# Two heads' row maxima side by side on TensorE, and one softmax shift for a pair of heads

## The chip, the cores and the metric

The kernel runs on one core of a Trainium2 chip. Its engines are TensorE (PE in the profile; PEld is its loading of weights), VectorE (DVE), ScalarE (ACT), GpSimd (POOL) and SyncE (SP, which here only issues DMAs). The metric is the time of one execution on the device, in microseconds, as the median of several runs.

## The reference

Attention with pooled queries is followed by a gated unit with a spatial product. B = 8, H = 8, 1152 keys, head size 64; two neighbouring queries are averaged, so there are 576 query rows.

```python
def _attn_ref(q, k, v):
    q_pool = q.reshape(B, H, S // 2, 2, D).mean(axis=3)
    scores = (1.0 / np.sqrt(D)) * np.matmul(q_pool, k.transpose(0, 1, 3, 2))
    scores = scores - np.max(scores, axis=-1, keepdims=True)
    attn = np.exp(scores)
    attn = attn / (np.sum(attn, axis=-1, keepdims=True) + 1e-09)
    return np.matmul(attn, v)

def _moe_ref(x, w_in, w_spatial, b_spatial, w_out):      # x: (8, 576, 512), heads joined
    h = np.maximum(x @ w_in, 0.0)
    u, v = h[..., :512], h[..., 512:]
    v_n = (v - mean(v)) / np.sqrt(var(v) + 1e-06)        # over the last axis
    v_s = np.einsum('ts,bsd->btd', w_spatial, v_n) + b_spatial[None, :, None]
    return (u * v_s) @ w_out
```

## The kernel before

**Pairs.** Two heads of a batch are worked on together as a pair; there are 32 pairs. A head's 576 query rows are cut into a main part of 512 and a tail of 64. Keys stand in 9 chunks of 128. Float32 precision is kept with float16 operands split into a high and a low part (`xq` or X, `khi`, `qhi`, `klo` or KL, `kn`; three sets of each, `kn` in one buffer).

**`prep(i)`** scales and splits queries and keys of pair i. X holds the high part of the queries, lower 64 partitions for head 0 and upper 64 for head 1; `kn` the high part of the keys in the same way. DMAs then copy them into `qhi` and `khi`, where a head's high and low parts lie over all 128 partitions; two small ones fill `qd`, a block-diagonal tile with the tails of both heads. `lnp` is the offset that the shift gets.

**`maxima(i)`** finds the largest score of each query row ahead of the exponentials. There are 9 row tiles (`t` 0 to 3 are head 0's main part, 4 both tails, 5 to 8 head 1's main part), each in three products of 128 query rows with 384 keys (L617; L608 for the tails). Each product goes to a PSUM bank, `pm` (two buffers) or `pw` (two buffers), of which `pw` is used only while no gated unit is running. VectorE reduces each (L623).

**`shift`** turns 4 or 5 columns of maxima into rows: a reduction (L635), the subtraction of `lnp` (L636), a transpose on TensorE (L640), the split in two float16 rows (L642, L643) and two DMAs into partitions 64 and 65 of X (L648). It is called twice for a pair, after tile 4 and after tile 8. Those two rows take part in the second score product: `products` multiplies the high parts (L793, 128 rows) and then KL with X (L794, 66 rows), which adds the low part of the keys and subtracts the shift.

**`attention(i)`** runs over 18 steps (2 heads, 9 chunks). In each, a score tile `pss` (L793, L794) goes through the exponential on ScalarE (L799) into one of 8 `pt` buffers, GpSimd splits it (L811), and two steps later `values` multiplies it with the values (L713, L717, L722; 12 small products a step). Tails are 64 columns wide and go through `tail_tile` and `tail_values`. While attention(i) runs, `maxima(i + 1)`, the values of the next pair, `prep(i + 2)` and the weights are advanced by generators.

**`gated_unit`** is the second half of the reference, for two batches at a time (L868 to L1058). A unit runs beside the next eight pairs; the last one runs alone at the end.

**Order.** Class `Order` records every instruction and its accesses, and `pin` then fixes each engine's order by list scheduling with a table of costs: the instruction that can start first, and among those the first in the program. The engines work through that order in sequence.

Of the kernel before, what the change touches and what calls it, by code (L numbers as in the profile page):

```python
# [10 lines left out]
F16 = mybir.dt.float16  # L11
# [20 lines left out]
class Order:  # L32
# [144 lines left out]

    def two_from_sbuf(self, ins):
        if ins.opcode not in ("TensorTensor", "TensorScalarPtr", "TensorCopy"):
            return False  # L180
        return not any(self.slot.get(x.bass_ap.tensor.name, (0, 0))[1] for x in ins.ins if hasattr(x, "bass_ap"))

    def pin(self, tc):
# [22 lines left out]
        cost = [self.cost(e, i) for e, i in zip(lane, prog)]  # L206
        shared = [e in ("DVE", "Pool") and self.two_from_sbuf(i) for e, i in zip(lane, prog)]
# [4 lines left out]
        wire = 0.0  # L212
# [3 lines left out]
        for _ in prog:  # L216
            best = None
            for e, ns in ready.items():
                if ns:
# [42 lines left out]
def attn_sgu_kernel(ctx: ExitStack, tc: tile.TileContext, qT, kT, v, w_in, w_spT, b_sp, w_out, out):  # L262
# [27 lines left out]
    pp = order.pool(ctx.enter_context(tc.tile_pool(name="pp", bufs=8)), 8)  # L290
# [35 lines left out]

    qd = [const.tile([P, 2, TAIL], F16, name=f"qd{i}") for i in range(2)]
    for t in qd:
        nc.gpsimd.memset(t, 0.0)

# [204 lines left out]
    def prep(i):  # L535
# [19 lines left out]
        nc.vector.scalar_tensor_tensor(  # L555
            out=lnp, in0=s[:, 0:1], scalar=math.log(PEXP) / ESC, in1=s[:, 1:2], op0=ALU.mult, op1=ALU.mult
        )
        nc.vector.tensor_scalar_min(lnp, lnp, 2.0 ** 29)
# [35 lines left out]
    def maxima(i):  # L594
        st = state[i]
        qhl, khh, X = st["qhl"], st["khh"], st["X"]
        W = KEYS // 3
        NB = W // P
        mt = sm.tile([P, NT, 3], F32, name="mt", bufs=2)
        for t in range(NT):  # L600
            for n in range(3):

                if units or (t + n) % 2:
                    pm = ps_m.tile([P, 512], F32, name="pm")
                else:
                    pm = ps_w.tile([P, 512], F32, name="pw")
                if t == 4:
                    nc.tensor.matmul(  # L608
                        pm[:, :W],
                        lhsT=qd[i % 2].rearrange("p h s -> p (h s)"),  # L610
                        rhs=st["kn"][:, n * NB : (n + 1) * NB, :],
                        start=True, stop=True,
                    )
                else:
                    h = 0 if t < 4 else 1
                    c0 = t * P if t < 4 else TAIL + (t - 5) * P
                    nc.tensor.matmul(  # L617
                        pm[:, :W],
                        lhsT=qhl[:, h, c0 : c0 + P],
                        rhs=khh[:, h, n * NB : (n + 1) * NB, :],  # L620
                        start=True, stop=True,
                    )
                nc.vector.reduce_max(out=mt[:, t, n : n + 1], in_=pm[:, :W], axis=AX.X)  # L623
                yield

            if t == 4:
                yield from shift(st, mt, 0, 5)
        yield
        yield from shift(st, mt, 5, NT)

    def shift(st, mt, a, z):
# [4 lines left out]
        nc.vector.tensor_scalar_sub(mx[:, :n], mx[:, :n], st["lnp"])  # L636
# [5 lines left out]
        nc.vector.tensor_scalar_mul(mr[:n, 0], pt[:n, :P], 1.0 / MROW)  # L642
        nc.vector.scalar_tensor_tensor(  # L643
# [532 lines left out]
```

## Time and profile before

| | |
|---|---|
| median of 3 runs | 1245.7 us (1244.05 to 1246.76) |
| the profiled execution | 1241.88 us, of which its span is 1240.1 us |
| mean granted TensorE clock | 0.979 |
| PE, DVE, ACT, POOL busy | 94%, 76%, 71%, 70% |
| chain that ended last | PE 70%, DVE 13%, ACT 3% |

"Busy" is a mean over stretches that differ. The prediction uses three of them: from 30 to 285 us pairs are worked on without a gated unit, from 285 to 1137 us with one, and from 1137 us the last unit runs alone. Matmuls are pipelined: a matmul's duration in the profile is longer than the distance to the next one's start, so distances between starts are read from the timeline.

### The profile page before, as it was taken

To read this page: it belongs to the slowest core of one execution; us is meant where nothing else is said; L and a number is where in the kernel's file an instruction comes from. 1 tells how busy PE (TensorE), PEld (TensorE's weight loads), DVE (VectorE), ACT (ScalarE), POOL (GpSimd) and SP (SyncE) were. 2 spreads that over 40 slices of the span, in tenths; PEclk is the share of its full clock that TensorE was granted. 3 is DMA by queue.
4 is the path that set the end of the run, shared out by engine and by line. 5 is a ranking of instruction groups with operands and counts; after the bars stand their busy time and mean duration, and the time that the engine had idled before them with its cause. 6 is when DMAs were issued, how large, how long until landed. Compare 5 with 4: busy or idle time off the path is not lost.

```text
span 1240.1 us, 34103 instructions
## 1 busy us (share of the span) xinstructions
PE 1165.3 (94%) x13632; PEld 732.9 (59%) x13632; DVE 941.6 (76%) x2219; ACT 885.1 (71%) x1627; POOL 872.4 (70%) x750
## 2 busy tenths in 40 slices
PE   3878879789999999999999999999999999999998
PEld 1555556556666666566666666666665666665454
DVE  5689999998878777876679777876669867841644
ACT  4677669778977787868677887768777786754333
POOL 2768969799878777778787777778877776774000
PEclk9879899899999999999999999999999999999999
DMA  5454364336333533155323432246332321110002
GB/s 186 161 167 137 90 199 120 110 90 198 92 109 78 147 112 104 53 137 165 106 74 93 131 95 68 74 128 186 109 91 74 90 70 50 33 44 36 1 1 77
DMA packets 62335, 126.70 MB, mean 102 GB/s; under 512 B 13728, under 2 KB 21920, under 8 KB 61664
## 3 DMA queue, kind: packets, MB, share of 16 engines
q1 hardware_dynamic: 62176, 124.52, 34.1%
q8 instruction: 107, 1.75, 0.6%
q14 instruction: 52, 0.43, 0.1%
HBM read 81.20 MB, written 9.44 MB: 73 GB/s over the span
## 4 chain that ended last, share of the span: by engine, by line
PE 70%; DVE 13%; ACT 3%; issue 2%; POOL 2%; DMA 1%; ACTq 0%; DVEq 0%; SPq 0%; POOLq 0%
PE pss L793 8%; PE pss L794 8%; PE pm L617 7%; PE pw L868 6%; PE pw L973 6%; PE pw L1016 6%; DVE mt L623 5%; PE pw L932 5%; PE o L713 4%; PE o L722 4%; PE o L717 4%; ACT pt L799 1%; PE pss L868 1%; PE pss L973 1%; DVE vv L372 1%
## 5 line engine op out<-in xcount | busy, mean ns | idle before, releaser
L811 POOL TENSOR_TENSOR pt<-pt 128x512 f16<-128x512 f32 x576 | 637.1, 1123 | 206.4 <-ACT pt L799 204.7
L799 ACT ACTIVATE pt<-pss,esc 128x512 f32<-128x512 f32 x576 | 387.1, 686 | 164.3 <-PE pss L794 122.4
L623 DVE TENSOR_REDUCE mt<-pm 128x1 f32<-128x384 f32 x733 | 385.7, 547 | 60.6 <-PE pm L617 52.4
L793 PE MATMUL pss<-qhi,khi 128*128 128x64 f16 (+1 forms) x1152 | 270.7, 289 | 13.5 <-ACT pt L799 11.2
L794 PE MATMUL pss<-xq,klo 66*128 66x64 f16 (+1 forms) x1152 | 275.8, 290 | 1.5 <-DMA xq<-mr 1.5
L713 PE MATMUL o<-vp,pt 128*128 128x65 f16 x2304 | 229.6, 196 | 0.0
L717 PE MATMUL o<-vp,pt 128*128 128x64 f16 x2304 | 227.6, 194 | 0.0
L617 PE MATMUL pm<-khi,qhi 128*128 128x384 f16 x655 | 206.0, 331 | 14.5 <-DVE mt L623 8.1
L713 PEld LDWEIGHTS <-pt 128*128 128x128 bf16 x2304 | 179.9, 99 | 46.6 <-issue 6.3
L717 PEld LDWEIGHTS <-pt 128*128 128x128 bf16 x2304 | 169.4, 99 | 31.7 <-issue 2.4
L722 PE MATMUL o<-vp,pt 128*128 128x65 f16 x2304 | 172.2, 195 | 0.9 <-POOL pt L811 0.7
L722 PEld LDWEIGHTS <-pt 128*128 128x128 f16 x2304 | 121.6, 99 | 26.2 <-POOL pt L811 4.0
L794 PEld LDWEIGHTS <-klo 66*128 66x128 f16 x1152 | 98.3, 99 | 51.5 <-issue 22.4
L617 PEld LDWEIGHTS <-qhi 128*128 128x128 f16 x768 | 74.7, 99 | 83.3 <-issue 36.2
L793 PEld LDWEIGHTS <-khi 128*128 128x128 f16 x1152 | 99.8, 99 | 30.7 <-issue 7.3
L868 PE MATMUL pw<-wi_h,xg 128*128 128x512 f16 x240 | 89.0, 378 | 0.0
L811 POOL TENSOR_TENSOR ptl<-ptl 128x1152 f16<-128x1152 f32 x32 | 71.3, 2230 | 19.6 <-ACT ptl L807 19.5
L807 ACT ACTIVATE ptl<-pss,esc 128x256 f32<-128x256 f32 (+1 forms) x128 | 63.7, 498 | 29.8 <-PE pss L794 29.4
L932 PE MATMUL pw<-xg,wi_h 128*128 128x512 f16 (+1 forms) x336 | 82.8, 325 | 0.0
L973 PE MATMUL pw<-ws_h,vv 128*128 128x512 f16 x216 | 80.5, 379 | 0.3 <-DVE u L983 0.3
L1016 PE MATMUL pw<-wo_h,vv 128*128 128x512 f16 x216 | 79.7, 379 | 0.8 <-DVE vv L372 0.8
L623 DVE TENSOR_REDUCE mt<-pw 128x1 f32<-128x384 f32 x131 | 70.1, 543 | 11.0 <-PE pw L617 10.5
(190 smaller groups left out, 2335.4 us busy)
## 6 DMA issues: line engine op xcount, KB each, us to landing
vt<-in_v_dram SPq DMA_DIRECT2D x56, 576.0 KB
qt<-in_qT_dram SPq DMA_DIRECT2D x32, 576.0 KB
kt<-in_kT_dram SPq DMA_DIRECT2D x32, 576.0 KB
khi<-kn SPq DMA_DIRECT2D x128, 144.0 KB
out_dram<-row SPq DMA_DIRECT2D x24, 256.0 KB
qhi<-xq SPq DMA_DIRECT2D x64, 72.0 KB
klo<-klo SPq DMA_DIRECT2D x32, 144.0 KB
vv<-in_w_in_dram SPq DMA_DIRECT2D x4, 1024.0 KB
```

Of the source, the lines that this page charges most:

```text
L617: nc.tensor.matmul(pm[:, :W], lhsT=qhl[:, h, c0 : c0 + P], rhs=khh[:, h, n * NB : (n + 1) * NB, :], start=True, stop=True,)
L623: nc.vector.reduce_max(out=mt[:, t, n : n + 1], in_=pm[:, :W], axis=AX.X)
L713: nc.tensor.matmul(o[:, t], lhsT=top[:, cols], rhs=vp[:, D : D + D1], start=c == 0 and t == 0, stop=False, skip_group_check=True,)
L717: nc.tensor.matmul(o[:, t, 0:D], lhsT=top[:, cols], rhs=vp[:, 0:D], start=False, stop=False, skip_group_check=True)
L722: nc.tensor.matmul(o[:, t], lhsT=rst[:, cols], rhs=vp[:, D : D + D1], start=False, stop=c == NC - 1, skip_group_check=True,)
L793: nc.tensor.matmul(o, lhsT=khh[:, h, c, :], rhs=qhl[:, h, q], start=True, stop=False)
L794: nc.tensor.matmul(o, lhsT=KL[0:KR, h, c, :], rhs=X[0:KR, h, q], start=False, stop=True)
L799: nc.scalar.activation(pt, ps, AF.Exp, bias=0.0, scale=esc)
L811: nc.gpsimd.tensor_sub(t.bitcast(F16)[..., 0::2], t, t.bitcast(BF16)[..., 1::2])
L868: nc.tensor.matmul(ph, lhsT=xa[:, cc, c0 : c0 + P], rhs=wa[:, cc, DH:DF], start=n == 0, stop=n == 3 * NCC - 1,)
L973: nc.tensor.matmul(pv, lhsT=l, rhs=r[:, 0:MAIN], **fl)
L1016: nc.tensor.matmul(py, lhsT=ga[:, fc, c0 : c0 + P], rhs=wa[:, fc, :], start=m == 0, stop=m == end - 1)
```

## The change

Six edits that go together:

1. Ahead of the maxima, the products read X and `kn` directly: 64 rows (the high part of the queries) where they had 128 (high and low part). For pairs 1 to 31, a product of head 0 (rows 0 to 63 of the array) and one of head 1 (rows 64 to 127) are issued one behind the other into two banks. For the tails both write one bank, 64 partitions each. Pair 0 keeps its products one at a time, and its two shifts. `qd` and its DMAs are gone; `kn` has two buffers, `pt` seven in place of eight.
2. The tails come first, then tiles 0 and 5 together, 1 and 6, and so on; `shift` is called once for all nine columns, at the end.
3. In `shift`, `lnp` is subtracted behind the transpose, on the row in PSUM; the split takes a copy and a subtraction.
4. `lnp` is made by an activation and one VectorE instruction in place of two on VectorE.
5. In `values` and `tail_tile`, the products into the same columns stand four or five apart and no longer next to each other.
6. `Order` learns that such products belong together: the first waits in the plan for what the second needs, the second follows at once, and the first is planned with 60 ns.

```diff
+        side = {
+            n - 1: n for n in range(1, len(prog))
+            if self.rows(prog[n - 1]) == (0, 64) and self.rows(prog[n]) == (64, 128)
+        }
+        for a, b in side.items():
+            before[a] |= before[b]
+            begun[a] |= begun[b] - {a}
+            begun[b].add(a)
...
+        for a in side:
+            cost[a] = (60, cost[a][1] + 60)
...
+            if beside is not None:
+                best = (free["PE"], "PE", beside)
             t, e, n = best
+            beside = side.get(n)
...
-    pp = order.pool(ctx.enter_context(tc.tile_pool(name="pp", bufs=8)), 8)
+    pp = order.pool(ctx.enter_context(tc.tile_pool(name="pp", bufs=7)), 7)
...
-        nc.vector.scalar_tensor_tensor(
-            out=lnp, in0=s[:, 0:1], scalar=math.log(PEXP) / ESC, in1=s[:, 1:2], op0=ALU.mult, op1=ALU.mult
+        nc.scalar.activation(lnp, s[:, 0:1], AF.Copy, bias=0.0, scale=s[:, 1:2])
+        nc.vector.tensor_scalar(
+            out=lnp, in0=lnp, scalar1=math.log(PEXP) / ESC, scalar2=2.0 ** 29, op0=ALU.mult, op1=ALU.min
         )
-        nc.vector.tensor_scalar_min(lnp, lnp, 2.0 ** 29)
...
-        for h, (a, rows) in enumerate(((MAIN, lower), (0, upper))):
-            nc.sync.dma_start(out=qd[i % 2][rows, h], in_=X[rows, 0, a : a + TAIL])
-        kn = st["kn"] = ld.tile([P, NC, P], F16, name="kn")
+        kn = st["kn"] = ld.tile([P, NC, P], F16, name="kn", bufs=2)
...
+        def product(o, h, c0, m, n):
+            nc.tensor.matmul(
+                o[:, :W],
+                lhsT=X[halves[h], 0, c0 : c0 + m],
+                rhs=kn[halves[h], n * NB : (n + 1) * NB, :],
+                start=True, stop=True,
+            )
+        def tails(n):
+            o = bank(n % 2)
+            for h in range(2):
+                product(o[halves[h]], h, MAIN * (1 - h), TAIL, n)
+            largest(4, n, o)
...
+        for n in range(3):
+            tails(n)
+            yield
+        for t in range(4):
+            for n in range(3):
+                os = [bank(h) for h in range(2)]
+                for h, o in enumerate(os):
+                    product(o, h, first(t + 5 * h), P, n)
+                for h, o in enumerate(os):
+                    largest(t + 5 * h, n, o)
+                    yield
+        yield
+        yield from shift(st, mt, 0, NT)
...
         nc.vector.reduce_max(out=mx[:, :n], in_=mt[:, a:z], axis=AX.X)
-        nc.vector.tensor_scalar_sub(mx[:, :n], mx[:, :n], st["lnp"])
...
-        nc.vector.tensor_scalar_mul(mr[:n, 0], pt[:n, :P], 1.0 / MROW)
-        nc.vector.scalar_tensor_tensor(
-            out=mr[:n, 1], in0=pt[:n, :P], scalar=1.0 / MROW, in1=mr[:n, 0], op0=ALU.mult, op1=ALU.subtract
+        m = pt[:n, :P]
+        nc.vector.tensor_scalar(
+            out=m, in0=m, scalar1=st["lnp"][:n], scalar2=1.0 / MROW, op0=ALU.subtract, op1=ALU.mult
         )
+        nc.vector.tensor_copy(out=mr[:n, 0], in_=m)
+        nc.vector.tensor_sub(mr[:n, 1], m, mr[:n, 0])
...
                 o[:, t], lhsT=top[:, cols], rhs=vp[:, D : D + D1], start=c == 0 and t == 0, stop=False,
                 skip_group_check=True,
             )
+        for t in range(4):
+            cols = slice(t * P, (t + 1) * P)
             nc.tensor.matmul(
                 o[:, t, 0:D], lhsT=top[:, cols], rhs=vp[:, 0:D], start=False, stop=False, skip_group_check=True
             )
```

What this makes of the order is shown at two places. The first is TensorE's order in the second stretch, inside a step of `values`, as it was. `pt` is the stationary operand of the value products, `qhi` that of a product for the maxima.

```order
L713 LDWEIGHTS pt
L713 MATMUL o<-vp_99,pt 128x65
L717 LDWEIGHTS pt
L717 MATMUL o<-vp_99,pt 128x64
L617 LDWEIGHTS qhi_117
L617 MATMUL pm<-khi_114,qhi_117 128x384
L713 LDWEIGHTS pt
L713 MATMUL o<-vp_99,pt 128x65
L717 LDWEIGHTS pt
L717 MATMUL o<-vp_99,pt 128x64
```

The same kind of place in the new order (L757 and L763 are what L713 and L717 were, L625 a product for the maxima; each product still has its own load of weights ahead of it):

```order
L757 LDWEIGHTS pt
L757 MATMUL o<-vp_100,pt 128x65
L625 LDWEIGHTS xq_112
L625 MATMUL pm<-kn,xq_112 128x384
L625 LDWEIGHTS xq_112
L625 MATMUL pm<-kn,xq_112 128x384
L757 LDWEIGHTS pt
L757 MATMUL o<-vp_100,pt 128x65
L757 LDWEIGHTS pt
L757 MATMUL o<-vp_100,pt 128x65
```

Two products for the maxima, both into `pm`, now stand one behind the other among value products, and L757 follows L757 where L717 stood between. Such products stand in exactly twos at 392 places of the new order, between instructions of full height, and in fours at 30.

The second place is VectorE's order in the first stretch, around a shift. Before (`mx` are the maxima, `mr` the rows made of them; L387, L372 and L555 belong to the weights, to `prep` and to `lnp`):

```order
L635 TENSOR_REDUCE mx<-mt 128x5
L555 SCALAR_TENSOR_TENSOR lnp<-qks 128x1
L636 TENSOR_SCALAR mx<-mx,lnp 128x5
L558 TENSOR_SCALAR lnp<-lnp 128x1
L642 TENSOR_SCALAR mr<-pm 5x128
L372 SCALAR_TENSOR_TENSOR qhi_118<-qt,qks,xq_112 128x576
L643 SCALAR_TENSOR_TENSOR mr<-pm,mr 5x128
```

And now (L678 is what L635 was; L685, L688 and L689 follow the transpose; L388, L412 are other work of `prep` and of the weights):

```order
L678 TENSOR_REDUCE mx<-mt 128x9
L388 SCALAR_TENSOR_TENSOR klo_106<-kt,qks,kn 128x512
L685 TENSOR_SCALAR pm<-pm,lnp 9x128
L412 TENSOR_TENSOR u<-u,vv 128x1024
L688 CAST mr<-pm 9x128
L633 TENSOR_REDUCE mt<-pm 128x1
L689 TENSOR_TENSOR mr<-pm,mr 9x128
```

The instruction with `lnp` stands behind the transpose and works on PSUM, all nine columns pass in one go, and other work stands between the three instructions of the row.

More of the change, by code (lines that the diff above doesn't have):

```diff
@@ L595, in maxima @@
         st = state[i]
-        qhl, khh, X = st["qhl"], st["khh"], st["X"]
+        X, kn = st["X"], st["kn"]
         W = KEYS // 3
         NB = W // P
+        halves = (slice(0, D), slice(D, P))
         mt = sm.tile([P, NT, 3], F32, name="mt", bufs=2)
-        for t in range(NT):
-            for n in range(3):
[L603 to L627, printed above, removed]
@@ new lines, in tails, with first @@
+        def tails(n):
[3 more added lines that the diff above has]
+            largest(4, n, o)
+        def first(t):
+            return t * P if t < 4 else TAIL + (t - 5) * P
+        if i == 0:
+            for t in range(NT):
+                for n in range(3):
+                    if t == 4:
+                        tails(n)
+                    else:
+                        o = bank((t + n) % 2)
+                        product(o, t // 5, first(t), P, n)
+                        largest(t, n, o)
+                    yield
+                if t == 4:
+                    yield from shift(st, mt, 0, 5)
+            yield
+            yield from shift(st, mt, 5, NT)
+            return
```

31 lines of the change are left out of this document (24 added, 7 removed).

## The prediction, made before the changed kernel was run

> **What bounds the kernel now.** I read the windows first, because the mean hides three stretches.
>
> ```profile
> 0.00:30.00 30.00, 10.01 (x32) 3.84 (x32) 17.22 (x43) 12.91 (x27) 7.57 (x16) 0.93 0.58 192
> 30.00:285.00 255.00, 214.39 (x2747) 141.98 (x2747) 230.13 (x500) 191.50 (x346) 206.75 (x162) 0.91 0.45 136
> 285.00:1137.00 852.00, 841.63 (x10262) 538.20 (x10259) 642.75 (x1558) 643.47 (x1184) 658.10 (x573) 1.00 0.34 98
> 1137.00:1241.00 104.00, 99.24 (x603) 48.85 (x598) 51.46 (x121) 37.25 (x72) 0.00 (x0) 1.00 0.08 26
> ```
>
> The columns are PE, PEld, DVE, ACT, POOL, clock, DMA. From 30 to 285 us VectorE is the busiest (230 of 255); from 285 to 1137 TensorE is busy 842 of 852 and the others 643 to 658; the last 104 us are the unit alone, which the change doesn't touch. A busy PE could still hide waits, so the waits of TensorE in the second stretch come next, then the timeline, which shows whether products follow each other as fast as they stream.
>
> ```profile
> PE pm L617 <- DVE mt L623: 4.2, 9, 1.1
> PE pm L617 <- DVE xt L771: 2.5, 3, 0.8
> PE pm L617 <- DVE rs L900: 1.0, 3, 0.4
> ```
>
> Its largest waits are 7.7 us together. So there each nanosecond of stream that goes is time, and in the first stretch a nanosecond of VectorE.
>
> ```profile
> 399.96 0.27 PE L640 MATMUL pm<-ident,mx 128*4 128x128 f32 x1
> 400.08 0.32 PE L617 MATMUL pm<-khi,qhi 128*128 128x384 f16 x1
> 400.24 0.38 PE L793 MATMUL pss<-qhi,khi 128*128 128x512 f16 x1
> ```
>
> A product for the maxima occupies 0.16 us (400.08 to 400.24), and its result comes another 0.16 later (duration 0.32).
>
> **The change part by part.** *Two heads side by side, second stretch.* It issues 552 full products for the maxima, those of 23 pairs of heads:
>
> ```profile
> 285.00:1137.00 852.00, 171.17 (x552) 52.95 (x552) 1.00 0.34 98
> ```
>
> That makes 276 twos and 69 tail products. No row of before has two products on different halves of the rows, so the price of a two needs bounds. Below, both start together: 0.16. Above, they don't overlap: 0.32, no gain. The nearest row is how closely two short products with a weight load each can start:
>
> ```profile
> 604.92 0.38 PE L868 MATMUL pw<-wi_h,xg 128*128 128x512 f16 x1
> 605.13 0.19 PE L713 MATMUL o<-vp,pt 128*128 128x65 f16 x1
> 605.16 0.19 PE L717 MATMUL o<-vp,pt 128*128 128x64 f16 x1
> 605.19 0.20 PE L713 MATMUL o<-vp,pt 128*128 128x65 f16 x1
> ...
> 605.35 0.19 PE L717 MATMUL o<-vp,pt 128*128 128x64 f16 x1
> ...
> 605.37 0.28 PE L722 MATMUL o<-vp,pt 128*128 128x65 f16 x4
> ```
>
> 0.03 apart. I take that: a two costs 0.19 and saves 0.13, 276 x 0.13 = -35.9 us. A load of weights takes 0.098:
>
> ```profile
> L617 PEld LDWEIGHTS <-qhi 128*128 128x128 f16 x552 | 53.0, 98 | 35.0 <-DVE xt L771 4.8 <-issue 0.2
> ```
>
> If the second load doesn't overlap the first product, a two costs 0.26 and saves 0.06: -16.6. The tails had one product (0.16) and get two: 69 x 0.03 = +2.1. The Trainium skill (TensorE: Matmul & The Clock Gate, Part 3, "The mechanism") has tiles of different row groups start some 4 ns apart; by that figure, as an estimate, a two would cost 0.164 and the term would be -43. No run here shows it yet.
>
> *One transpose less a pair:* 23 x 0.12 (399.96 to 400.08) = -2.8.
>
> *Columns apart.* Eight products L713 and L717 take 0.24 (605.13 to 605.37). Four of L722, whose columns differ, take 0.28 with the last one's duration:
>
> ```profile
> L722 PE MATMUL o<-vp,pt 128*128 128x65 f16 x2304 | 172.2, 195 | 0.9 <-POOL pt L811 0.7
> ```
>
> (0.28 - 0.195)/3 = 0.028 apart, so eight would take 0.23: 0.01 for each of 24 x 18 steps = -4.3; the rounding of the rows leaves 0 to -8. For the tail tiles, of which the same holds, I take 0.
>
> Stream of the second stretch: -35.9 + 2.1 - 2.8 - 4.3 = -40.9.
>
> *New waits there.* A two wants both `pm` banks, so both reductions of the two before it must be over. Today a product waits 7.7/552 = 0.014 on average; I give each two twice that, 276 x 0.028 = +7.7. Queued behind a waiting two is everything on TensorE, since its order is fixed; who waits for it are the exponentials. Ends 0 and +30: a tenth of the longest of those waits (1.1) for each two. The shift now ends with the last column of both heads and the next pair's first L794 needs it; before, the first half was ready half a pair earlier. From transpose to that product was:
>
> ```profile
> 27.82 0.37 PE L640 MATMUL pm<-ident,mx 128*5 128x128 f32 x1
> 28.70 0.80 PE L617 MATMUL pm<-khi,qhi 128*128 128x384 f16 x2 [0.50 <-DVE vs L356]
> 29.83 0.48 PE L617 MATMUL pm<-khi,qhi 128*128 128x384 f16 x1 [0.33 <-DVE mt L623]
> 31.25 1.01 PE L794 MATMUL pss<-xq,klo 66*128 66x512 f16 x2 [0.94 <-DMA xq<-mr]
> ```
>
> 3.4 us, with one more instruction on VectorE 3.7. Counted in the new order with the distances above, 3.7 to 6.4 us of products stand between them in the second stretch: mostly covered, +4. The same ends hold it. Second stretch: -40.9 + 11.7 = -29.
>
> *VectorE, first stretch.* The instructions that go or shrink, in the window 30 to 285 us:
>
> ```profile
> L636 DVE TENSOR_SCALAR mx<-mx,lnp 128x5 f32<-128x5 f32 x8 | 6.1, 766 | 0.0
> L636 DVE TENSOR_SCALAR mx<-mx,lnp 128x4 f32<-128x4 f32 x8 | 4.7, 591 | 0.0
> L555 DVE SCALAR_TENSOR_TENSOR lnp<-qks 128x1 f32<-128x1 f32 x9 | 4.5, 504 | 0.0
> L771 DVE TENSOR_SCALAR xt<-pm,dent 64x64 f32<-64x64 f32 x16 | 4.5, 278 | 0.1
> ...
> L642 DVE TENSOR_SCALAR mr<-pm 4x128 f16<-4x128 f32 x8 | 2.2, 278 | 4.8 <-PE pm L640 4.7
> L642 DVE TENSOR_SCALAR mr<-pm 5x128 f16<-5x128 f32 x8 | 2.2, 277 | 1.9 <-PE pm L640 1.9
> L643 DVE SCALAR_TENSOR_TENSOR mr<-pm,mr 5x128 f16<-5x128 f32 x8 | 2.2, 271 | 0.0
> L643 DVE SCALAR_TENSOR_TENSOR mr<-pm,mr 4x128 f16<-4x128 f32 x8 | 2.2, 270 | 0.0
> ```
>
> L636 takes 591 to 766 ns for five elements, while L771, with a per-partition operand too but from PSUM, takes 278 for 64. So the subtraction behind the transpose should cost about 0.28: 10.8 goes; L555 (4.5) goes to ScalarE, as one activation a pair beside 191 of 255 busy; the row of maxima was 8.8 and becomes 3 x 0.28 x 8 = 6.7. Together -17.4 of VectorE. At a busy share of 230/255 that is -15.7; against it stands the shift at the end of the pair, where only 2 to 3.5 us of products cover the 3.7 (+1 a pair, and other VectorE work stands within the three instructions). I take -12; ends -17.4 and 0. Seven `pt` buffers in place of eight belong to the same ends. In this stretch ScalarE waits for a buffer:
>
> ```profile
> ACT pt L799 <- PE o L722: 26.5, 7, 6.0
> ```
>
> These 7 waits get longer, but ScalarE has 63 us to spare here; if that cover is gone, they cost up to the 12.
>
> *Start.* VectorE stands still once while keys are copied for the products of pair 1:
>
> ```profile
> 40.19 1.54 DVE L372 SCALAR_TENSOR_TENSOR klo<-kt,qks,kn 128x640 f16<-128x640 f32 x2
> 46.22 0.56 DVE L623 TENSOR_REDUCE mt<-pw 128x1 f32<-128x384 f32 x1 [4.49 <-PE pw L617]
> ```
>
> Products that read `kn` need no copy: -4.5. The first products of all start earlier too, but VectorE's order then waits for the squares of the values, whose DMA lands no sooner:
>
> ```profile
> 24.21 0.68 ACT L366 ACTIVATE ws_l<-xg 128x576 f16<-128x576 f32 x1 [8.81 <-DMA xg<-in_v_dram]
> ```
>
> So 0 there. On SP 64 DMAs for `qd` and 62 for the rows go: off the path, 0.
>
> Sum: -29 - 12 - 4.5 = -45.5, from 1241.9 for the profiled execution to 1196.4. The median of the runs shown lies 3.8 above that execution, so I forecast 1200.
>
> **The rivals.** *Changing the shape of the array drains it* (slower). A two stands alone between products of full height, so each has two changes. If each had to wait until results are out, it would cost the 0.16 by which a product's duration exceeds its spacing: 2 x 0.16 a two, 345 twos with the tails: +110 us, and the sum ends at 1200 + 110 = 1310. It decides from 45.5/(345 x 2) = 0.07 us a change. Against it: L640, whose weights are 4 or 5 columns and which the built program puts on a 128x32 part, starts and is followed without such a gap, 0.12 us to L617 above, while full transposes are 0.11 apart:
>
> ```profile
> 367.04 0.60 PE L744 MATMUL pm<-ident,xm 128*128 128x128 f32 x4
> 367.48 0.38 PE L932 MATMUL pw<-xg,wi_h 128*128 128x512 f16 x1
> ```
>
> (0.44/4). That is a change by columns, though, not by rows. The Trainium skill (TensorEngine Tiling, "Key Properties") says that changing the tiling mode drains TensorE, which is this rival; the row of L640 doesn't bear it out.
>
> *The two don't overlap* (no change in effect). Then the twos give 0 and the tails +69 x 0.16 = 11: second stretch +11 - 7.1 + 11.7 = +15.6, with -16.5 elsewhere 1245. The products go to different banks and different rows, which speaks against it; nothing in the trace decides.
>
> *The overlap works, but the two banks are the new bound*. `pm` is also taken by transposes, tail values and shifts, and VectorE waits for L767 and for L640 already:
>
> ```profile
> DVE dent L692 <- PE pm L767: 37.8, 21, 12.7
> DVE mr L642 <- PE pm L640: 32.3, 35, 2.2
> ```
>
> A wait of 0.11 a two (+30 in place of +7.7) gives 1222.
>
> **How the numbers follow.** My forecast with few waits has 0.62, banks as the bound 0.13, no overlap 0.12, drains 0.13. The likeliest alone: stream -51 (both start together) to -17 (0.26 a two, tails too), waits 0 to +30, first stretch and start -22 to 0, not all at one end: 1179 to 1228. The range goes up over the banks' 1222 and part of the case without overlap: 1179 to 1240. About 0.2% (2.5 us) is what a measurement can tell from no change. Faster: 0.62 + 0.13 + 0.03 of the case without overlap = 0.78. The same: 0.06 of that case; slower: its last 0.03 and the 0.13 = 0.16.
>
> **What the profile after would show.** Right: in the second stretch twos of L625 with the next product 0.19 after the first; the stretch some 30 us shorter with TensorE still above 95%; no row like L636; the first stretch over near 268 us. Wrong: 0.3 or more from a two to the next product (no overlap), 0.5 (drains), long waits of L625 for L633 (banks) or of L840 for the DMA of `mr` (shift).

## The result, and the profile after

The change made the kernel slower: 1281.3 us (median of 4 runs, 1279.9 to 1282.7) against 1244.9 for the kernel before on the same chip, a ratio of 1.030 [1.027, 1.032]. The profiled execution of after has a span of 1278.1 us. The forecast was 1200, range 1179 to 1240. What happened is the rival by which a change of the array's shape costs time, at a smaller price a change than it assumed, and with a loss in the first stretch that it did not count.

The windows of after, with their ends moved to where the three stretches now end (columns as in the prediction: PE, PEld, DVE, ACT, POOL, clock, DMA):

```profile
0.00:30.00 30.00, 9.74 (x33) 3.46 (x34) 16.56 (x38) 15.39 (x31) 7.27 (x14) 1.00 0.58 192
30.00:307.00 277.00, 230.72 (x2771) 139.19 (x2769) 230.09 (x465) 193.38 (x350) 206.57 (x160) 0.86 0.42 127
307.00:1174.00 867.00, 859.06 (x10284) 494.99 (x10281) 601.67 (x1441) 651.09 (x1208) 655.17 (x575) 1.00 0.33 95
1174.00:1278.00 104.00, 100.38 (x622) 49.64 (x618) 51.48 (x121) 37.28 (x72) 0.73 (x1) 1.00 0.08 26
```

(This trace has no record of the clock before 41.5 us, so the 1.00 of its first row says nothing.) The first stretch became 22 us longer and the second 15; the last 104 us did not move. TensorE is still busy 859 of 867 us in the second stretch, so it does not look as if it waited for anything. In that stretch the products of the maxima alone (the same view, filtered to L625):

```profile
307.00:1174.00 867.00, 119.93 (x690) 34.27 (x690) 1.00 0.33 95
```

They are busy for 120 us, tails included. Before, the 552 full products were busy for 171 and the 69 tails (L608) for 21 more:

```profile
285.00:1137.00 852.00, 21.41 (x69) 6.69 (x69) 1.00 0.34 98
```

By these rows the change gained 73 us; the stretch lost 15. The loss therefore does not show in busy time, and only starts show it. TensorE in the timeline of after (start, duration, count at the end):

```profile
357.53 0.38 PE L839 MATMUL pss<-qhi,khi 128*128 128x512 f16 x1
357.75 0.38 PE L840 MATMUL pss<-xq,klo 66*128 66x512 f16 x1
358.07 0.34 PE L625 MATMUL pm<-kn,xq 64*128 64x384 f16 x2
358.33 0.39 PE L922 MATMUL pw<-wi_h,xg 128*128 128x512 f16 x1
358.56 0.38 PE L922 MATMUL pw<-wi_l,xg 128*128 128x512 f16 x1
```

Between full products of 512 columns starts are 0.22 apart (357.53 to 357.75). From the last one to the two it is 0.32, and 0.26 from the two to the next product, 0.16 of which is the stream of 384 columns. So a two waits 0.10 when it begins and the next product 0.10 when it is over. This change between products on the whole array and products on a part of it is called a border from here on. The line of L625 counts both products and lasts 0.34 where one lasts 0.333: the second starts 3 ns behind the first. The weight loads of the same place:

```profile
357.54 0.10 PEld L840 LDWEIGHTS <-klo 66*128 66x128 f16 x1
358.06 0.10 PEld L625 LDWEIGHTS <-xq 64*128 64x128 f16 x2 [0.43 <-issue]
358.33 0.33 PEld L922 LDWEIGHTS <-xg 128*128 128x128 f16 x3 [0.17 <-issue]
```

L840's load starts at 357.54, 0.2 ahead of its product (357.75). The loads of the two, and the first load behind it, start only with their products: nothing is loaded ahead across the border. And where two twos stand in a row:

```profile
227.27 0.22 PE L763 MATMUL o<-vp,pt 128*128 128x64 f16 x2
227.43 0.33 PE L625 MATMUL pm<-kn,xq 64*128 64x384 f16 x1
227.43 0.33 PE L625 MATMUL pw<-kn,xq 64*128 64x384 f16 x1
227.60 0.32 PE L625 MATMUL pm<-kn,xq 64*128 64x384 f16 x1
227.60 0.32 PE L625 MATMUL pw<-kn,xq 64*128 64x384 f16 x1
227.86 0.23 PE L763 MATMUL o<-vp,pt 128*128 128x64 f16 x2
```

The second two starts 0.17 behind the first: half rows behind half rows pay nothing. That is the overlap that was forecast, and the border is the cost that was not.

Waits for banks, which the forecast put at 7.7 us more than before, became fewer. TensorE's largest waits in the second stretch of after:

```profile
PE pm L625 <- DVE xt L817: 2.4, 3, 1.2
PE pm L625 <- DVE mt L633: 1.7, 3, 0.7
PE pss L840 <- DMA xq<-mr: 1.2, 2, 0.8
```

### The profile page after: what moved, and what is told of

Same layout as the page of the kernel before. It is cut to its first block, busy times and chain, and to the rows that moved or that the text cites. A ratio compares the mean times of both kernels' runs of the same rounds, so it can differ in the third digit from the quotient of the medians.

```text
span 1278.1 us, 33803 instructions
## 1 busy us (share of the span) xinstructions
PE 1199.9 (94%) x13697; PEld 687.3 (54%) x13697; DVE 899.8 (70%) x2063; ACT 897.1 (70%) x1659; POOL 869.8 (68%) x748
## 4 chain that ended last, share of the span: by engine, by line
PE 77%; DVE 14%; ACT 2%; POOL 1%; issue 1%; DMA 1%; SPq 0%; ACTq 0%; DVEq 0%
PE pss L840 8%; PE pss L839 8%; PE pm L625 8%; PE pw L1027 7%; PE pw L922 6%; PE pw L1070 6%; PE pw L986 5%; DVE mt L633 5%; PE o L757 5%; PE o L768 5%; PE o L763 5%; PE pss L856 1%; PE pss L922 1%; PE pss L852 1%; PE pm L790 1%; PE pss L1027 1%
## 5 line engine op out<-in xcount | busy, mean ns | idle before, releaser
L839 PE MATMUL pss<-qhi,khi 128*128 128x512 f16 x576 | 225.4, 392 | 7.6 <-ACT pt L845 7.4
L840 PE MATMUL pss<-xq,klo 66*128 66x512 f16 x576 | 224.3, 396 | 2.2 <-DMA xq<-mr 2.2
L625 PE MATMUL pm<-kn,xq 64*128 64x384 f16 (+1 forms) x826 | 167.1, 343 | 23.7 <-DVE mt L633 10.0
L757 PE MATMUL o<-vp,pt 128*128 128x65 f16 x2304 | 173.9, 196 | 6.8 <-DVE xm L776 6.8
L763 PE MATMUL o<-vp,pt 128*128 128x64 f16 x2304 | 172.3, 196 | 0.0
L768 PE MATMUL o<-vp,pt 128*128 128x65 f16 x2304 | 170.9, 196 | 0.3 <-POOL pt L865 0.3
L757 PEld LDWEIGHTS <-pt 128*128 128x128 bf16 x2304 | 128.7, 100 | 77.3 <-issue 12.7
L625 PEld LDWEIGHTS <-xq 64*128 64x128 f16 (+1 forms) x960 | 50.7, 96 | 158.7 <-issue 140.5
L763 PEld LDWEIGHTS <-pt 128*128 128x128 bf16 x2304 | 113.2, 99 | 7.3 <-issue 6.0
L840 PEld LDWEIGHTS <-klo 66*128 66x128 f16 x576 | 56.6, 100 | 32.3 <-issue 20.8
L839 PEld LDWEIGHTS <-khi 128*128 128x128 f16 x576 | 57.2, 99 | 25.0 <-issue 13.4
L542 POOL TENSOR_TENSOR vp<-vt,vp 128x576 f16<-128x576 f32 x48 | 60.0, 1250 | 15.2 <-ACT vp L540 15.0
```

Source lines behind the costliest of these rows:

```text
L625: nc.tensor.matmul(o[:, :W], lhsT=X[halves[h], 0, c0 : c0 + m], rhs=kn[halves[h], n * NB : (n + 1) * NB, :], start=True, stop=True,)
L757: nc.tensor.matmul(o[:, t], lhsT=top[:, cols], rhs=vp[:, D : D + D1], start=c == 0 and t == 0, stop=False, skip_group_check=True,)
L763: nc.tensor.matmul(o[:, t, 0:D], lhsT=top[:, cols], rhs=vp[:, 0:D], start=False, stop=False, skip_group_check=True)
L768: nc.tensor.matmul(o[:, t], lhsT=rst[:, cols], rhs=vp[:, D : D + D1], start=False, stop=c == NC - 1, skip_group_check=True,)
L839: nc.tensor.matmul(o, lhsT=khh[:, h, c, :], rhs=qhl[:, h, q], start=True, stop=False)
L840: nc.tensor.matmul(o, lhsT=KL[0:KR, h, c, :], rhs=X[0:KR, h, q], start=False, stop=True)
```

## The experiments

Stretches are measured here from the first main score product of pair 0 to that of pair 8, and from there to that of pair 31, read off the timeline of each profiled execution, in us. The times are medians, each compared with runs of the kernel before taken together with it (medians 1242.7 to 1245.0). Two columns say more of the first stretch: how long TensorE stood idle between its products (waits), and for how long the trace records a granted clock of 0.5 (half clock; no trace here records any value but 0.5 and 1.0).

| kernel | time | ratio to before | first stretch | second | waits, first | half clock, first |
|---|---|---|---|---|---|---|
| before | 1244.9 | | 265.8 | 821.8 | 45.0 | 51 |
| after | 1281.3 | 1.030 [1.027, 1.032] | 290.8 | 836.2 | 55.3 | 79 |
| full-height products (e1) | 1231.8 | 0.993 [0.991, 0.995] | 260.2 | 817.2 | 46.2 | 41 |
| columns apart alone (e2) | 1239.3 | 0.998 [0.996, 1.000] | 267.6 | 820.9 | 45.2 | 58 |
| factor alone (e3) | 1228.5 | 0.989 [0.987, 0.991] | 257.9 | 815.6 | 43.3 | 38 |
| columns and factor (e4) | 1225.9 | 0.988 [0.985, 0.991] | 258.9 | 817.3 | 44.7 | 38 |
| planner told the price (e5) | 1278.3 | 1.027 [1.023, 1.032] | 286.2 | 842.5 | 49.3 | 79 |
| seven `pt` alone (e6) | 1248.6 | 1.004 [1.002, 1.006] | 271.7 | 821.6 | 45.4 | 61 |
| tails at full height (e7) | 1265.0 | 1.016 [1.010, 1.022] | 284.6 | 829.4 | 53.8 | 72 |
| two twos in a row (e9) | 1277.5 | 1.029 [1.025, 1.032] | 290.5 | 834.2 | 55.7 | 92 |
| twos in second stretch only (e11) | 1251.8 | 1.008 [1.005, 1.011] | 260.7 | 839.8 | 45.3 | 44 |
| full height, kept together (e12) | 1240.2 | 0.996 [0.994, 0.999] | 268.0 | 818.7 | 52.1 | 41 |

The stretches are those of one execution for each kernel, and runs of one kernel differ (those of before lie between 1238.0 and 1251.5), so a few us in one stretch prove little by themselves. In after, e5, e7 and e9 the record of the clock begins at 41.5 to 44.9 us, in the others at 19 to 22. The products of 512 columns ahead of it start 0.40 us apart or more, as at half clock, so the last column is some 25 to 28 us too small for these four and 2 to 4 for the others.

**Full-height products.** After, with the products of the maxima back on 128 rows:

```diff
-                lhsT=X[halves[h], 0, c0 : c0 + m],
-                rhs=kn[halves[h], n * NB : (n + 1) * NB, :],
+                lhsT=st["qhl"][:, h, c0 : c0 + m],
+                rhs=st["khh"][:, h, n * NB : (n + 1) * NB, :],
```

(and one product from `qd` for the tails).

> The changed kernel with one part undone: the products for the maxima use all 128 rows again (qhi and khi, and qd with its DMAs for the tails), in the changed kernel's sequence, with one shift for a pair, lnp behind the transpose, columns apart and seven pt buffers. Theory A (a product on half the rows makes TensorE drain before and after it): the second stretch (pairs 8 to 31) loses about 276 x 0.05 + 69 x 0.23 = 30 us against the changed kernel, from 836 to about 806, and TensorE shows no gap of 0.31 ahead of such a product. Theory B (the 24 us lost in the first stretch come from drains too): the first stretch falls from 307 to below 285, the whole below 1230 us. Rival C (the first stretch lost them to the shift that now ends late, to the new sequence or to the pt buffer): the first stretch stays above 295, the whole at about 1250 us.

It took 1231.8: the half rows, together with the order that keeps two of them side by side, cost 49.5 us, and everything else in the change together gained about 11. Both stretches lose by them: 30.6 in the first, 19.0 in the second.

**Columns apart, and the factor, alone and together.** Each put into before:

```diff
+        for t in range(4):
+            cols = slice(t * P, (t + 1) * P)
             nc.tensor.matmul(
                 o[:, t, 0:D], lhsT=top[:, cols], rhs=vp[:, 0:D], start=False, stop=False, skip_group_check=True
...
```

```diff
-        nc.vector.tensor_scalar_sub(mx[:, :n], mx[:, :n], st["lnp"])
...
+        nc.vector.tensor_scalar(
+            out=m, in0=m, scalar1=st["lnp"][:n], scalar2=1.0 / MROW, op0=ALU.subtract, op1=ALU.mult
+        )
```

> The kernel before with only the columns apart (values and tail_tile). If same columns next to each other cost 0.003 a product, as unrounded starts in the trace of before suggest, the second stretch gains 3 to 6 us: 1239 to 1242 us against 1245. If it is nothing, 1245 within 2 us.

> The kernel before with only lnp subtracted behind the transpose and lnp made on ScalarE; two shifts, full rows. If VectorE bounds the first stretch, its 15 us less there bring 8 to 15 us: 1230 to 1237 us. If the first stretch is bound by chains across engines rather than VectorE's work, less than 4 us: above 1241.

> The kernel before with both: columns apart and lnp behind the transpose; two shifts, full rows, eight pt buffers. If the two gains add up: 1226 to 1234 us. If the fixed order reacts more strongly than the gains, it can land anywhere within 10 us of before.

Columns apart gained 3.9 us of medians, with an interval of 0.5 to 4.9; its one profiled execution is no shorter than that of before (1240.9 and 1240.1). The factor gained 14.6: 7.9 in the first stretch, with 14 us less at half clock, and 6.2 in the second, where none was forecast. Together they make 1225.9, the fastest kernel here: 1.2% [0.9, 1.5] below before, with 128 rows, two shifts a pair and eight `pt` buffers.

**The price of the products by themselves.** TensorE alone, patterns of a 512-column product and what is to be priced, 20 times each, at a granted clock of 1.00 (called the price kernel below):

> Price of the disputed products by themselves: TensorE alone, no engine to wait for, patterns of 20 repeats each, every product to the next of 8 banks; nothing of the reference is computed. Theory A (TensorE drains when products go from full height to half rows, or back): a 512-column product to the first of a two 0.31 us in place of 0.215, second 0.003 later, next full product 0.265 after that, so a two 0.37 against 0.33 for two full products; two twos in a row add only 0.17, four add 0.17 each; a lone half-row product costs as much as a two; a two of 64 columns pays the same 0.1 at entry and a like amount at exit. Theory B (no drain: the weights of the other half cannot be loaded ahead, so a load is exposed): the gap at entry follows the number of weight columns, 0.098 for 128, about a quarter for 32. Theory C (what after showed were waits for banks): no gap here, 0.19 from the first of a two to the next product. Products of 32 columns at full height (a change by columns): A as the prediction read it, no gap, 0.16; if any change of shape drains, 0.31 and 0.27 as for the twos.

All products come from one line, so the view of that line is taken for the time of each pattern. A row gives the count, shortest, median and longest duration in ns, first and last start in us, and the forms. Each window is cut from one 512-column product to the eighteenth after it:

```profile
L52 PE MATMUL o<-k,w x55: 326/326/379, 37.4 to 47.1; 128*128 128x384 f16 x36, 128*128 128x512 f16 x19
L52 PE MATMUL o<-k,w x55: 332/333/390, 48.3 to 58.9; 64*128 64x384 f16 x36, 128*128 128x512 f16 x19
L52 PE MATMUL o<-k,w x91: 322/333/389, 60.3 to 73.8; 64*128 64x384 f16 x72, 128*128 128x512 f16 x19
L52 PE MATMUL o<-k,w x37: 332/389/390, 96.7 to 107.3; 128*128 128x512 f16 x19, 64*128 64x384 f16 x18
L52 PE MATMUL o<-k,w x37: 336/389/390, 120.5 to 131.1; 128*128 128x512 f16 x19, 128*32 128x384 f16 x18
L52 PE MATMUL o<-k,w x55: 332/333/390, 140.4 to 151.0; 64*32 64x384 f16 x36, 128*128 128x512 f16 x19
```

Eighteen rounds with two full products took 9.7 us, 0.54 each. With a two in their place it was 10.6, or 0.59: the two costs 0.05 *more* than what it replaces. Two twos in a row: 13.5, or 0.75, while four full products would be 0.54 + 2 x 0.163 = 0.87: 0.11 cheaper. A lone half-row product costs as much as a two (10.6). So the price belongs to the border, not to the product. It doesn't follow the weight load either: with 32 weight columns in place of 128 the round takes the same 10.6, where theory B expected the gap to shrink to a quarter. And a product on all 128 rows but 32 columns (the fifth row) pays it in the same way, 10.6 too: a change by columns pays as well. The prediction held the opposite, on the word of L640.

**Which forms escape.** L640 has few weight columns too, and no gap stood there. Short products of 128 columns behind each 512-column product:

> Which changes by columns drain: one short product of 128 columns after each 512-column product, TensorE alone, 20 each of: full transpose in f32; transposes of 4 columns in f32 (as L640) and in f16; plain products with 4 weight columns in f32 and f16; 32 and 64 weight columns in f16; 66 rows; full height. Nothing of the reference is computed. Theory A (every change of the part's size drains, and L640 escapes because it is a transpose): plain products on 128x32 and 128x64 parts 0.32 after the 512-column product, transposes 0.216. Theory G (L640 escapes because it is f32): f32 0.216, f16 0.32. 66 rows and full height 0.216 in both.

From its timeline, transposes of 4 columns in f32 (L85 with `ident`), in f16 (L85 with `ident_h`), and plain f32 products of 4 columns (L89):

```profile
36.69 0.38 PE L52 MATMUL o<-k,w 128*128 128x512 f16 x1
36.90 0.27 PE L85 MATMUL o<-ident,kf 128*4 128x128 f32 x1
37.01 0.38 PE L52 MATMUL o<-k,w 128*128 128x512 f16 x1
...
43.90 0.39 PE L52 MATMUL o<-k,w 128*128 128x512 f16 x1
44.22 0.22 PE L85 MATMUL o<-ident_h,k 128*4 128x128 f16 x1
44.37 0.39 PE L52 MATMUL o<-k,w 128*128 128x512 f16 x1
...
53.49 0.39 PE L52 MATMUL o<-k,w 128*128 128x512 f16 x1
53.80 0.27 PE L89 MATMUL o<-ident,kf 128*4 128x128 f32 x1
```

The f32 transpose starts 0.21 behind the long product (36.69 to 36.90) and is followed 0.11 later: no border. The f16 transpose starts after 0.32, the plain f32 product after 0.31. So neither theory held: being a transpose is not enough, nor being f32. Plain f16 products with 4, 32 or 64 weight columns start after 0.32 too; those of 128 columns, on 66 rows or on all, after 0.22. So of the forms with few weight columns only the f32 transpose goes free, and L640 is exactly that. It is spaced as a full f32 transpose is (0.22 and 0.11). Why isn't shown: the views give its 4 columns, but not on which part of the array it ran.

**Tails.** After, with the tails in one full-height product:

```diff
-            for h in range(2):
-                product(o[halves[h]], h, MAIN * (1 - h), TAIL, n)
+            nc.tensor.matmul(
+                o[:, :W],
+                lhsT=qd[i % 2].rearrange("p h s -> p (h s)"),
+                rhs=kn[:, n * NB : (n + 1) * NB, :],
+                start=True, stop=True,
+            )
```

> After with its tails as one full-height product from qd, as before had them; the twos of full columns stay. Theory A (each change of height costs): a tail costs 0.388 where a full product costs 0.162, 0.23 each; 69 in the second stretch -10 to -16 (where a tail stands beside a two it saves less), 27 in the first -4 to -6: about 1262. Rival (the twos alone carry the loss, tails hide in it): 1275 to 1281.

1265.0: the tails alone cost 16 us of medians and 12 of the two profiled spans (1278.1 and 1265.9): 6.8 in the second stretch, less than the 10 expected, and 6.2 in the first. They replaced one product by two and pay the borders for it. (In the second stretch of this trace TensorE also waits 2.9 us longer than in after, and 6.8 us ran at half clock, where after has none.)

**Is it the order?** The planner was told 60 ns for the first product of a two. It got the measured price:

```diff
-            cost[a] = (60, cost[a][1] + 60)
+            cost[a] = (98, cost[a][1] + 98)
+            cost[b] = (277, cost[b][1])
```

> After with the planner told what a two costs (98 and 277 ns of TensorE in place of 60 and a full product); the same instructions, in another order. Theory A (the array itself takes the time): second stretch the same within 3 us, first stretch at most 8 us shorter, 1273 to 1282. Rival D (the order, planned for twos that are too cheap, makes VectorE and the exponentials late, above all in the first stretch): it gets back 15 or more of the 25 us lost there, 1265 or less.

1278.3: the first stretch gains 4.6, the second loses 6.3, which is more than the 3 that theory A allowed. An order planned with the measured price does not get the time back; that no other order would isn't shown.

**The first stretch.** It lost more (30.6) with fewer products for the maxima (260 against 690), so three kernels ask why. First half rows only while a unit runs:

```diff
-                lhsT=X[halves[h], 0, c0 : c0 + m],
+                lhsT=X[halves[h], 0, c0 : c0 + m] if units else st["qhl"][:, h, c0 : c0 + m],
...
```

> After with half-row products only once the unit runs; full-height products before that. Theory A (each stretch loses its own time): first stretch as with full-height products, 260 us, second stretch 836: 1251, 1247 to 1255. Rival F (what one stretch loses the next makes up, or carries on): second stretch away from 836 by 6 or more, below 1245 or above 1257.

1251.8, with 260.7 in the first stretch and 839.8 in the second, 3.6 more than in after (6.8 us of it ran at half clock): the losses are local and add up. Then two twos in a row where four banks are free, which was meant to halve the borders:

```diff
...
+            now = [left.pop(0) for _ in range(1 if units else min(2, len(left)))]
+            os = [(t, n, h, bank(len(now) > 1 and k)) for k, (t, n) in enumerate(now) for h in range(2)]
...
```

> After with two twos in a row (four products, four banks) in the first stretch where no unit holds the banks; the second stretch keeps single twos. The array's prices as the products by themselves showed: one two between full products 0.05 us dearer than two full ones, two twos in a row 0.11 cheaper than four full ones. Theory A (the first stretch lost its time to the changes of height): it has half the changes and gets back half or more of the 24 us that the twos lost there, 1269 or less. Rival E (the loss there comes from the lower clock and from waits on VectorE for banks, not from the changes): four banks must now be free at once, no gain or a loss, 1277 or more.

1277.5, and the first stretch stayed at 290.5. Theory A's 12 us did not come. But the borders were not halved either: half-row products stand at 76 places of the stretch where after has 101, since after had fours already, and tails and pair 0 kept theirs. And the half clock grew to 92 us. Its timeline shows both what was meant and what came in between (TensorE, then VectorE at the second place):

```profile
88.38 0.38 PE L841 MATMUL pss<-xq,klo 66*128 66x512 f16 x1
88.69 0.34 PE L625 MATMUL pm<-kn,xq 64*128 64x384 f16 x2
88.86 0.33 PE L625 MATMUL pw<-kn,xq 64*128 64x384 f16 x2
89.12 0.29 PE L853 MATMUL pss<-qhi,khi 128*128 128x64 f16 x4
...
138.35 0.78 PE L625 MATMUL pm<-kn,xq 64*128 64x384 f16 x2
139.12 0.94 PE L625 MATMUL pw<-kn,xq 64*128 64x384 f16 x2
141.63 0.27 PE L812 MATMUL pm<-vp,ptl 128*128 128x130 f16 x1 [1.57 <-DVE mt L633]
```

```profile
137.59 1.01 DVE L633 TENSOR_REDUCE mt<-pm 128x1 f32<-128x384 f32 x2
138.53 1.00 DVE L633 TENSOR_REDUCE mt<-pw 128x1 f32<-128x384 f32 x2
...
139.52 1.58 DVE L388 SCALAR_TENSOR_TENSOR klo<-kt,qks,kn 128x512 f16<-128x512 f32 x1
```

At 88.69 four products take 0.17 and 0.26. At 138.35 they come one by one, 0.31 to 0.47 apart, while the clock is at half from 138.2 on; two reductions take 1.0, and a split of keys of 1.58 stands before the next. Meanwhile TensorE waits 1.57. So the last part was to keep two heads' products together, with two banks at once, but at full height:

```diff
-            if self.rows(prog[n - 1]) == (0, 64) and self.rows(prog[n]) == (64, 128)
+            if prog[n - 1].name in self.one and prog[n].name in self.other
...
```

(the planner's 60 ns are out as well, and the tails are one product).

> The kernel with full-height products (after's order and reads otherwise) with one thing put back: the two heads' products of a column are kept side by side in TensorE's order and wait for both their banks, as the twos do; no change of height anywhere. Two twos in a row halved the changes in the first stretch and it stayed at 290 us, so something else carries the 24 us there. Rival E1 (keeping them together, two banks at once, does): first stretch 275 to 285 in place of 260, second 817 to 825, 1250 to 1262. Rival E2 (the half rows do, by a lower clock or their drains where the clock is low): first stretch 260 to 265, 1230 to 1240.

1240.2, 268.0 in the first stretch: between the two theories' bands. Keeping them together costs 7.8 of the 30.6 there (and 1.5 in the second stretch), 5.9 of it as waits. The half rows, tails included, cost the larger part, 22.8.

The starts of all TensorE instructions of after and of the full-height kernel say where it stands. In the second stretch the clock is 1.00 in both. Around the half-row products (from the start of the product ahead of them to the start of the one behind, less waits) after spends 183.4 us, at 333 places. The full-height kernel spends 183.7 around its products for the maxima, but these stand alone more often, at 537 places, and the 204 more products ahead of them take some 23 by themselves. So the half rows cost about 23 there. Waits are 6.1 fewer, other spacing adds about 2, and that makes the measured 19.0. A single two takes 0.384 on average, less waits.

In the first stretch the same sum says something else. After spends 73.5 around the half-row products, the full-height kernel 79.7, of which its 57 more places take 7: about the same. TensorE's waits are 9.1 more, and the other 21 us stand at products that have nothing to do with the maxima. They run at a lower granted clock. The stretch from 30 to 285 us of after, of the full-height kernel and of the kernel kept together:

```profile
30.00:285.00 255.00, 209.36 (x2469) 125.48 (x2468) 215.07 (x425) 172.72 (x311) 187.08 (x143) 0.85 0.41 127
30.00:285.00 255.00, 209.88 (x2795) 138.24 (x2794) 227.55 (x475) 199.33 (x362) 212.99 (x165) 0.93 0.47 141
30.00:285.00 255.00, 206.21 (x2740) 137.17 (x2739) 223.82 (x467) 192.00 (x351) 202.56 (x160) 0.93 0.46 137
```

0.85 against 0.93 with the same busy time: TensorE did 2469 products in the time of 2795, and 0.08 of 255 us is 20 us. Two neighbouring windows of after show how it looks, TensorE busy in all of both:

```profile
116.00:120.00 4.00, 4.00 (x30) 2.04 (x30) 3.95 (x8) 3.09 (x7) 3.38 (x4) 0.50 0.44 184
120.00:124.00 4.00, 4.00 (x59) 2.42 (x58) 3.02 (x6) 3.83 (x8) 2.19 (x2) 1.00 0.01 4
```

In the first, products of 512 columns start 0.41 apart (116.55 to 116.96), where at full clock it is 0.22. Sorted by the clock at their start, products away from the maxima lose 27 us of the first stretch to the half clock in after and 8 in the full-height kernel: 19 us. It isn't one execution's accident: the mean clock was 0.965 to 0.969 in all four runs of after, and 0.977 to 0.983 in all seven of the full-height kernel.

Why the clock is lower isn't shown. The four kernels with half rows in this stretch have the most time at half clock (72 to 92 us), but seven buffers alone, without half rows, have 61. In the price kernel, where TensorE never waits, the clock stayed 1.00 with a border at every product, so borders alone do not lower it; nor do waits alone, since the kernel kept together waits 52 us where after waits 55, and has 41 us at half clock.

**Seven buffers.** Before with one `pt` buffer fewer:

```diff
-    pp = order.pool(ctx.enter_context(tc.tile_pool(name="pp", bufs=8)), 8)
+    pp = order.pool(ctx.enter_context(tc.tile_pool(name="pp", bufs=7)), 7)
```

> Before with seven pt buffers in place of eight, nothing else. After with full-height products took 1231.8 and before with the columns apart and the factor 1225.9; 5.9 us are left for one shift a pair, kn in two buffers and seven pt buffers. If the buffers carry it: 1243 to 1249, mainly in the first stretch. If the one shift carries it: 1243 within 2.

1248.6, and its trace has 5.9 us more in the first stretch, with 10 us more at half clock. ScalarE's wait for L722, which frees the buffers, grows from 26.5 to 33.2 between 30 and 285 us. So the buffers can account for what e1 lacks to e4 (5.9 us of medians, 1.1 between the two profiled executions); that the one shift a pair costs nothing isn't shown.

## Why the prediction was wrong

Two steps failed. The first is the price of a two. The prediction took it from the nearest row, two short products 0.03 apart, which made 0.19, and bounded it by 0.16 and 0.32. It was 0.375 by itself and 0.384 in the kernel, outside those bounds, because no row of before had a border, and both ends assumed none. The rival that named the border was given 0.13, against it stood one row, L640; that row was the only form tried with few columns that pays nothing. The second is the first stretch: the cost of the half rows there was put at nothing without a row, and with the order that goes with them they cost 30.6.

Of the 84 us between the forecast for the profiled execution (1196.4) and its time (1279.9), 43 stand in the second stretch and about as many in the first. In the second, twos and tails alone were off by some 62; waits that fell where they were to grow hid 14 of it.

Step by step, in the order of the sum:

- *Bound.* TensorE bounds the second stretch, and each nanosecond of it is time: right, about 23 us more around the twos and tails than with full-height products came out as 19.0.
- *Twos, -35.9.* In the second stretch the 276 twos took 0.384 on average, where two full products at the price kernel's spacing take 0.326: +16. The overlap itself was better than forecast (3 ns between the two where 30 were taken); the Trainium skill (TensorE: Matmul & The Clock Gate, Part 3, "The mechanism") gives 4 ns, and the trace agrees. What it doesn't price is the border, 0.106 us on the way in (0.322 from a 512-column product in place of 0.216) and 0.103 on the way out (0.266 in place of 0.163) in the price kernel.
- *Tails, +2.1.* They cost +12.7 around them, six times the term: 45 of the 69 stand alone and pay both borders for a product that got no shorter, and 24 stand in twelve pairs that share them.
- *The rival.* It decides from 0.07 us a change, and a change cost 0.10. Its own price, 0.16 a change, was taken from a duration and too high. With 0.21 a two its sum would be 1200 + 345 x 0.21 = 1272; that the measured 1281 lies so near is in part luck, since that sum has nothing for the first stretch. The sign from a two to the next product (0.5 for drains) did not come either: it was 0.26. The Trainium skill (TensorEngine Tiling (Array Packing), "Key Properties") says that changing the tiling mode drains TensorE. The prediction set the row of L640 against that rule; the price kernel agrees with the rule for rows and for columns, and the run of forms shows the one exception tried, the f32 transpose.
- *Waits, +7.7 and +4.* The first has the wrong sign: L617 waited 7.7 us for VectorE in the second stretch, L625 waits about 4. L840 waits 1.2 for the shift's DMA: right in sign, and smaller.
- *Columns, -4.3.* Alone it gained 3.9 (0.5 to 4.9). In its one trace the spacing of the second stretch is 2.6 shorter, against 1.7 more in waits: right in kind.
- *First stretch, -12.* Half right. The factor alone gained 7.9 there, and full-height products with everything else 5.6. L636 is gone, as forecast, and its successor takes 0.34 where 0.28 was taken:

```profile
L685 DVE TENSOR_SCALAR pm<-pm,lnp 9x128 f32<-9x128 f32 x7 | 2.4, 344 | 1.2 <-PE pm L682 1.2
```

But the half rows, which were summed only for the second stretch, cost 30.6 in this one with their order. The prediction treated this stretch as VectorE's alone, so that products on TensorE were free there. They were not: some 20 us went with the lower granted clock, and 9 are waits.
- *Seven buffers, 0.* They cost 3.6 us (1.9 to 7.7). The wait that the prediction named, and put down as covered by ScalarE's spare time, grew by 6.7.
- *Start, -4.5.* The first pair begins 1.3 us earlier (16.1 in place of 17.4), but from there to pair 1 it takes 37.7 in place of 32.2, and 3.6 of the 5.5 more are waits. The full-height kernel takes 33.6, so most of it goes with the half rows; products run at half speed until 41.5 us there, until 36 in before.
- *Second stretch of the factor, 0.* It gained 6.2 that no term had: by the starts of all TensorE instructions 2.1 in waits and 4.1 in the spacing of products. L640's waits for L636 were 0.6 us there, too little for it; the cause is open.

## What to carry to other kernels

Before a product is moved to a part of the array, count the borders: each change between part and whole costs some 0.10 us of TensorE at full clock, whatever the number of weight columns, the f32 transpose apart, so one two of 384 columns (0.16 saved, 0.21 paid) loses, two in a row win 0.11 by themselves, and a product that only gets split loses at once. Look for the price in the distance between starts around the product, since its own busy time will look like a gain; and when a rule says that something stalls and one row says it doesn't, find out in which forms the row differs before giving it the word. A stretch in which another engine is busiest is not free for TensorE either, so compare the granted clock stretch by stretch: here some 19 of the 31 us lost in the first stretch went with a lower clock at products that the change did not touch.

## What the runs showed of the hardware that was not expected

- A change of part costs the same by rows (64x128), by columns (128x32), with 32 or 128 weight columns: a round of 0.59 us where the same stream without a border takes 0.38 (512 and 384 columns).
- Moving between the two halves of the rows costs nothing: the second product of a two starts 3 ns later, a second two 0.17 later.
- An f32 transpose of 4 columns pays no border (0.22 to it, 0.11 behind it, as a full f32 transpose); an f16 transpose of the same shape pays it on both sides (0.32 and 0.15, where a full f16 product of 128 columns has 0.06).
- Borders without waits left the granted clock at 1.00 (price kernel), and 52 us of waits without borders left 41 us of the first stretch at half clock. With both, after has 55 us of waits and at least 79 us at half clock there. What lowers the clock stays open.
